# Narrowing a third of the gated layer's weights beside the attention and keeping them in DRAM

## The chip, the cores and the metric

One Trainium2 chip, one of its cores. The metric is device time in microseconds of one execution; below it stands as the median of three runs, beside one execution that was profiled. The engines are called TensorE (PE in the profile, its weight loads PEld), VectorE (DVE), ScalarE (ACT), GpSimd (POOL) and SyncE (SP, which here only issues DMAs).

## What is computed

Attention in both directions between 512 rows and 32 states for 8 x 8 heads of 64, then a mixture of eight experts with one expert per row, then a gated layer (`moe2`):

```python
attn_out = _attn_ref(**attn_kwargs)                  # (8, 8, 544, 64)
x = attn_out.transpose(0, 2, 1, 3).reshape(4608, 512)
# experts: argmax of normalised logits, out[mask] = gate * relu(x[mask] @ w1[e]) @ w2[e]
x = _moe_ref(x=x, **moe_kwargs)
# gated layer, d_ff = 1536
g = x @ w_gate
silu = g * (1.0 / (1.0 + np.exp(-g)))
val = x @ w_val
out = (silu * val @ w_out).astype(np.float32)
```

The three weights of the gated layer arrive as float64 (`wide` in the code), as pairs of 32-bit words. The kernel has no float64 arithmetic: it narrows a tile to float32 by integer operations on the two words.

## The kernel before

Each product is made of three float32r matmuls (`mm3`, lines 138 to 140), for which every operand is split into a high and a low part (`split`: ScalarE copies the high part, line 127; VectorE or GpSimd subtracts for the low one, line 131).

**Order.** The order of all instructions is made by hand. `Streams` runs a main stream and several side streams: each `yield` of the main stream is one round, in which every side stream takes one step; a side stream that yields a number k sits out k rounds, and one that yields a function stands until it is true. `groups` is the first main stream: 64 expert rounds n (8 for each of 8 batches b), each with the products `ph` (then `hH` on ScalarE, `hL` on VectorE, lines 616 and 617) and, for the round before, `acc`; the weights of experts are fetched on SP and split in between, and every other round has `states_w1`. An expert round has about 7 yields; n = 0 has four fewer than the others of its kind. Beside it run `attn_a` for two halves q (lines 244 to 319; the last is started once batch 5 has begun, sits out `a_off` rounds, and adds one to `done_a` at its end), `attn_b`, `route`, and `later`.

**later** (line 1054) waits until all 16 parts of `attn_a` are done, closes their pool `ap`, routes the state rows (`slots_route`), then runs `weights2` and after it the experts of the state rows (`slots`), which run beside the rest of the gated layer.

**weights2** (line 878) prepares 36 tiles: for each f of 12 the tiles g, v and o (128 x 512). A tile is loaded on SP (line 895, 512 KB, three raw buffers), squared on ScalarE (line 918), narrowed by four VectorE instructions (`narrow`, lines 871, 873, 875, 876), and split one iteration later, the low part on GpSimd. `c_gap` sets the rounds between: 4 while experts run, 2 once `w2b` is open. From f = 2 on a tile also waits for a function, which costs a round.

**moe2** (line 956) is the second main stream: 8 units of 512 rows and one of 256, each with 12 steps f of pg, pv and, for the step before, o: 36 matmuls of 512 columns and 12 yields. A step can be placed only when its three tiles have been split. During the first unit the tiles of f = 4 to 11 are still being made; as long as they are, the low part `yL` of the product is made on GpSimd, else on VectorE. The buffer `sg` is single.

Of the kernel before, what the change touches and what calls it, by code (L numbers as in the profile page):

```python
# [9 lines left out]
F32 = mybir.dt.float32  # L10
F32R = mybir.dt.float32r
BF16 = mybir.dt.bfloat16
I32 = mybir.dt.int32
AF = mybir.ActivationFunctionType
# [12 lines left out]
NCA = 2  # L27
# [53 lines left out]
class W:  # L81
# [25 lines left out]
    c_mask = "vector"  # L107
    c_gap = (0, 4, 2)
    c_lo = ("pool",)


class Kernel:
# [30 lines left out]
    def setup(self, cp, kp, dp):  # L143
        nc = self.nc
        for i in range(2):
            self.zp.tile([128, 512], F32, tag="sst", name=f"sst{i}", bufs=2)
        self.bds = [[cp.tile([128, 2, 128], F32, name=f"bd{q}_{i}") for i in range(NBD)] for q in range(2)]
        for i in range(NBD):
            for q in range(2):
                nc.vector.memset(self.bds[q][i], 0.0)  # L150
        for q in range(2):
            self.load_bd(0, q)
            self.load_x(0, q)
        for q in range(2):
            self.load_bd(1, q)
        self.tauv = cp.tile([128, 32], F32, name="tauv")[:, 0:1]
        nc.sync.dma_start(self.tauv, self.tau.to_broadcast([128, 1]))
        self.em = self.zp.tile([8, DM], F32, tag="sq", name="em", bufs=2)
        nc.sync.dma_start(self.em, self.emb)
        self.ident = kp.tile([128, 128], F32, name="ident")  # L160
        make_identity(nc, self.ident)
        self.bs = [[cp.tile([128, 2, 128], F32R, name=f"bs{k}{q}") for k in "HL"] for q in range(2)]
        one = self.zp.tile([128, 512], F32, tag="sq", name="one", bufs=2)[:, :128]
        nc.gpsimd.memset(one, 1.0)
        self.ones = kp.tile([128, 128], F32R, name="ones")
        nc.vector.tensor_copy(self.ones, one)
        self.rev = cp.tile([128, 4, 8], F32, name="rev")
        for e in range(E):
            nc.gpsimd.memset(self.rev[:, :, e:e + 1], float(E - e))
        kc = cp.tile([128, 2], F32, name="kc")  # L170
        nc.gpsimd.memset(kc[:, 0:1], 0.5)
        nc.gpsimd.memset(kc[:, 1:2], math.e)
        self.half = kc[:, 0:1]
        self.euler = kc[:, 1:2].unsqueeze(2)
        self.enT = cp.tile([128, 4, 16], F32R, name="enT")
        self.tri_b = cp.tile([128, 128], BF16, name="tri_b")
        self.ones_b = cp.tile([128, 128], BF16, name="ones_b")
        self.iota = self.zp.tile([128, 512], F32, tag="iota", name="iota", bufs=1)
        self.rtau = cp.tile([128, 1], F32, name="rtau")
        self.ess = cp.tile([8, 1], F32, name="ess")  # L180
        self.en = cp.tile([8, 1], F32, name="en")

        cp.tile([128, 32], F32, name="fill_c")
        self.xs = [self.zp.tile([128, DM], F32, tag="xs", name=f"xs{t}", bufs=2) for t in range(2)]
        self.goh = kp.tile([128, 36, 8], F32, name="goh")
        self.ov = kp.tile([128, 9], F32, name="ov")
        self.ovi = kp.tile([128, 10], I32, name="ovi")
        kp.tile([128, 24], F32, name="fill_k")
        self.x2d = dp.tile([9, 128, 4, 512], F32, name="x2d")
        self.x1d = dp.tile([9, 2, 128, 4, 512], F32R, name="x1d")  # L190
        self.ec = kp.tile([128, NCHK], I32, name="ec")
        self.gm8 = kp.tile([128, 256], F32, name="gm8")
        self.xsld = dp.tile([NCHK, 128, 512], F32R, name="xsld")
        self.seltd = dp.tile([128, 1024], F32R, name="seltd")
        self.x2sd = dp.tile([2, 128, 4, 512], F32R, name="x2sd")
        self.gohd = dp.tile([9, 128, 4, 8], F32, name="gohd")
        self.gm, self.eb, self.scS, self.bdT, self.at, self.PT, self.ss = {}, {}, {}, {}, {}, {}, {}
# [664 lines left out]
            yield W.s_gap[2]  # L862


    def narrow(self, raw, t, q):

        nc = self.nc
        lo, hi = raw[:, :, 0], raw[:, :, 1]  # L870
        getattr(nc, W.c_mask).scalar_tensor_tensor(t.bitcast(F32), t.bitcast(F32), LEAST_SQ, hi.bitcast(F32),  # L871
                                       op0=ALU.is_ge, op1=ALU.mult)
        nc.vector.tensor_scalar(q, t, 3, 0x3FFFFFFF, op0=ALU.logical_shift_left, op1=ALU.bitwise_and)  # L873
        yield W.c_gap[0]
        nc.vector.scalar_tensor_tensor(t, t, -0x40000000, q, op0=ALU.bitwise_and, op1=ALU.bitwise_or)  # L875
        nc.vector.scalar_tensor_tensor(q, lo, 29, t, op0=ALU.logical_shift_right, op1=ALU.bitwise_or)  # L876

    def weights2(self):

        nc, cv = self.nc, self.cv  # L880
        todo = [(f, nm) for f in range(NC2) for nm in "gvo"]
        N = len(todo)
        raw, sq, val = {}, {}, {}

        def load(i):
            if i >= N:
                return
            f, nm = todo[i]
            fs = slice(f * 128, f * 128 + 128)
            k = " k" if self.wide else ""  # L890
            src = {"g": self.wg, "v": self.wv, "o": self.wo}[nm]
            src = src[fs] if nm == "o" else src[:, fs].rearrange(f"(c p) f{k} -> p c f{k}", p=128)
            shape = [128, 512, 2] if self.wide else [128, 512]
            raw[i] = cv.tile(shape, I32 if self.wide else F32, tag="raw", name=f"raw{nm}{f}", bufs=3)
            nc.sync.dma_start(raw[i] if nm == "o" else raw[i].rearrange(f"p (c f){k} -> p c f{k}", c=4), src)

        load(0)
        load(1)
        yield 4
        for i in range(N + 2):  # L900
            m = i - 2
            if m >= 0:
                f, nm = todo[m]
                if f < NCA:
                    h, l = [self.w2a.tile([128, 512], F32R, tag=f"{nm}{k}{f}", name=f"{nm}{k}{f}") for k in "HL"]
                elif f < NCA + NCT:
                    yield lambda: not self.routing
                    tags = TAKEN[2 * (m - 3 * NCA):][:2]
                    h, l = [self.zp.tile([128, 512], F32R, tag=t, name=f"{nm}{k}{f}", bufs=BUFS[t])
                            for k, t in zip("HL", tags)]  # L910
                else:
                    yield lambda: self.w2b is not None
                    h, l = [self.w2b.tile([128, 512], F32R, tag=f"{nm}{k}{f}", name=f"{nm}{k}{f}") for k in "HL"]
                self.split(h, l, val.pop(m), lo_eng=W.c_lo[m % len(W.c_lo)])
                self.W2.setdefault(f, []).extend((h, l))
            if i < N and self.wide:
                sq[i] = cv.tile([128, 512], I32, tag="t64", name=f"t{i}", bufs=2)
                nc.scalar.activation(sq[i].bitcast(F32), raw[i][:, :, 1].bitcast(F32), AF.Square)
            m = i - 1
            if 0 <= m < N:  # L920
                if self.wide:
                    q = cv.tile([128, 512], I32, tag="q64", name=f"q{m}", bufs=2)
                    yield from self.narrow(raw.pop(m), sq.pop(m), q)
                    val[m] = q.bitcast(F32)
                else:
                    val[m] = raw.pop(m)
            load(i + 2)
            yield W.c_gap[1 if self.w2b is None else 2]
# [81 lines left out]
    def run(self):  # L1010
# [9 lines left out]
        def close(*keys):  # L1020
            for k in keys:
                open_.pop(k).close()
# [11 lines left out]
        cp = pool("cp", 1, "right")  # L1034
        self.wp = pool("wp", 2, "right")
        self.hp = pool("hp", 2, "right")
        self.raw, self.regs, self.fetched, self.cuts, self.done_a, self.xr = {}, {}, [0, 0], [0, 0], 0, {}
        self.en_done = self.scored = False
        st = Streams()
        self.spreading, self.slots_done, self.begun = False, False, set()  # L1040
        self.W2, self.x2, self.x2r, self.w2b, self.routing = {}, [], {}, None, True
# [6 lines left out]
        def routes():  # L1048
# [2 lines left out]
                yield from self.route(b)  # L1051
            self.routing = False

        def later():

            yield lambda: self.done_a == 16
            close("ap")
            self.lp = pool("lp", reuse_waits="tile")
            yield from self.slots_route()
            close("lp")  # L1060
# [33 lines left out]
        with tc.manual_schedule():  # L1094
            self.setup(cp, kp, dp)
            for q in range(2):
                st.add(self.start_pace(self.attn_a(q), W.p_a))
            st.add(self.start_pace(attn_b(), W.p_b))
            st.add(self.setup_route())
            st.add(self.start_pace(routes(), W.p_r))  # L1100
            st.add(later())
            st.run(main())
        close("lp", "x2p", "gp", "ps")
        self.general(pool, close)
# [119 lines left out]
```

## Time and profile before

| | us |
|---|---|
| median of 3 runs | 1520.24 (1518.88 to 1521.37) |
| the profiled execution | 1522.9 |
| its span, first to last instruction | 1521.4 |
| PE busy | 1423.9 (94%) |
| DVE busy | 853.0 (56%) |
| ACT busy | 572.9 (38%) |
| POOL busy | 284.3 (19%) |

The shares are means over stages that differ. In the page's 40 slices of 38 us each TensorE's digit is 9 nearly throughout; it is 7 or 8 only in slices 12 to 18, and 4 and 6 in the first two. VectorE's digit is 5 to 8 up to slice 13, 9 in the next four, 8 in slice 18, and 2 to 4 after it, mostly. Of the DMA traffic, 120.91 of 132.53 MB goes through the queue of SP.

### The profile page before, as it was taken

What the parts mean: (1) busy time and instruction counts of PE and PEld (TensorE: products, weight loads), DVE (VectorE), ACT (ScalarE), POOL (GpSimd) and SP (SyncE); (2) the same over time, 40 slices, a digit from 0 to 9 for tenths busy, and PEclk for the clock granted to TensorE, in tenths of its full rate; (3) what the DMA queues carried; (4) which work ended last, traced back from release to release, by engine and by line L of the source; (5) the groups of instructions that cost most, each with busy time, mean ns of one, the idle gap of its engine ahead of it and who ended that gap; (6) DMA issues with size and microseconds to landing.
All of it is one profiled execution on the core that took longest, in us unless ns stands there. A gap on an engine that the chain in (4) does not pass through costs nothing.

```text
span 1521.4 us, 20615 instructions
## 1 busy us (share of the span) xinstructions
PE 1423.9 (94%) x6997; PEld 1167.1 (77%) x6998; DVE 853.0 (56%) x1725; ACT 572.9 (38%) x1195; POOL 284.3 (19%) x254
## 2 busy tenths in 40 slices
PE   4699999999988788889999999999999999999997
PEld 4577877878877576668888888888888888888887
DVE  5568687677785999984443444344344443443232
ACT  3455554544644433333332333233242332332121
POOL 2224334343343335430000000000000000000100
PEclk8799999999999999999999999999999999999999
DMA  3333233333244543332222132132131231231210
GB/s 75 100 83 107 90 113 121 103 106 104 71 145 144 173 134 111 125 112 72 60 70 76 60 90 77 42 101 65 36 111 49 62 105 41 74 94 35 90 40 16
DMA packets 134818, 132.53 MB, mean 87 GB/s; under 512 B 45736, under 2 KB 109736, under 8 KB 134448
## 3 DMA queue, kind: packets, MB, share of 16 engines
q1 hardware_dynamic: 128992, 120.91, 26.2%
q0 software_dynamic: 5520, 9.96, 2.4%
q8 instruction: 57, 0.93, 0.3%
q14 instruction: 57, 0.47, 0.1%
q10 hardware_dynamic: 192, 0.26, 0.1%
HBM read 108.54 MB, written 31.98 MB: 92 GB/s over the span
## 4 chain that ended last, share of the span: by engine, by line
PE 53%; DVE 10%; issue 2%; DMA 2%; ACT 1%; POOL 1%; SPq 0%; DVEq 0%; ACTq 0%; POOLq 0%
PE pg L138 5%; PE pv L138 5%; PE pg L139 5%; PE pg L140 5%; PE o L140 5%; PE o L139 5%; PE pv L139 5%; PE pv L140 5%; PE o L138 5%; DVE t L875 2%; DVE t L871 2%; DVE q L873 2%; PE psl L803 1%; DVE q L876 1%; PE psl L804 1%
## 5 line engine op out<-in xcount | busy, mean ns | idle before, releaser
L138 PE MATMUL pg<-x2H,gH 128*128 128x512 f32 (+1 forms) x432 | 167.6, 388 | 12.6 <-DVE sg L985 12.4
L985 DVE TENSOR_TENSOR sg<-pg,sg 128x512 f32<-128x512 f32 (+1 forms) x108 | 71.4, 661 | 182.1 <-ACT sg L984 181.8
L138 PE MATMUL pv<-x2H,vH 128*128 128x512 f32 (+1 forms) x432 | 166.0, 384 | 3.1 <-DVE sg L987 3.1
L139 PE MATMUL pg<-x2L,gH 128*128 128x512 f32 (+1 forms) x432 | 166.0, 384 | 0.2 <-DVE x2L L131 0.2
L140 PE MATMUL pg<-x2H,gL 128*128 128x512 f32 (+1 forms) x432 | 165.9, 384 | 0.0
L140 PE MATMUL pv<-x2H,vL 128*128 128x512 f32 (+1 forms) x432 | 164.8, 381 | 0.0
L139 PE MATMUL pv<-x2L,vH 128*128 128x512 f32 (+1 forms) x432 | 164.7, 381 | 0.0
L140 PE MATMUL o<-oH,yL 128*128 128x512 f32 x408 | 160.5, 393 | 0.0
L139 PE MATMUL o<-oL,yH 128*128 128x512 f32 x408 | 160.3, 393 | 0.0
L138 PE MATMUL o<-oH,yH 128*128 128x512 f32 x408 | 160.3, 393 | 0.0
L127 ACT ACTIVATE yH<-sg 128x512 fp32r<-128x512 f32 (+1 forms) x108 | 65.7, 609 | 237.1 <-DVE sg L987 237.1
L131 DVE TENSOR_TENSOR swL<-sraw,swH 128x256 fp32r<-128x256 f32 x256 | 102.7, 424 | 52.8 <-ACT swH L127 51.1
L984 ACT ACTIVATE sg<-pg 128x512 f32<-128x512 f32 (+1 forms) x108 | 61.9, 573 | 184.8 <-PE pg L140 181.1
L127 ACT ACTIVATE swH<-sraw 128x256 fp32r<-128x256 f32 x256 | 99.3, 410 | 63.5 <-PE sacc L830 38.2
L139 PE MATMUL acc<-hL,w1H 128*128 128x512 f32 x256 | 103.4, 404 | 15.1 <-DVE hL L617 15.1
L138 PE MATMUL acc<-hH,w1H 128*128 128x512 f32 x256 | 107.1, 418 | 9.5 <-ACT w1H L127 9.1
L987 DVE TENSOR_TENSOR sg<-pv,sg 128x512 f32<-128x512 f32 (+1 forms) x108 | 71.3, 660 | 76.6 <-PE pv L140 76.1
L140 PE MATMUL acc<-hH,w1L 128*128 128x512 f32 x256 | 103.4, 404 | 1.5 <-DVE w1L L131 0.9
L138 PEld LDWEIGHTS pg<-x2H,gH 128*128 128x128 f32 x432 | 81.8, 189 | 29.6 <-DVE sg L985 15.8
L131 DVE TENSOR_TENSOR yL<-sg,yH 128x512 fp32r<-128x512 f32 (+1 forms) x98 | 64.7, 660 | 65.9 <-ACT yH L127 65.9
L138 PEld LDWEIGHTS pv<-x2H,vH 128*128 128x128 f32 x432 | 81.3, 188 | 18.4 <-DVE sg L987 4.5
L140 PEld LDWEIGHTS pg<-x2H,gL 128*128 128x128 f32 x432 | 82.0, 190 | 17.1
(290 smaller groups left out, 3014.3 us busy)
## 6 DMA issues: line engine op xcount, KB each, us to landing
sraw<-in_moe_w SPq DMA_DIRECT2D x256, 128.0 KB
raw<-in_moe_w SPq DMA_DIRECT2D x32, 512.0 KB
raw<-in_moe_w SPq DMA_DIRECT2D x64, 256.0 KB
xr<-in_x SPq DMA_DIRECT2D x64, 128.0 KB
x2d<-xo SPq DMA_DIRECT2D x32, 256.0 KB
x2r<-x2d SPq DMA_DIRECT2D x32, 256.0 KB
out<-ob SPq DMA_DIRECT2D x32, 256.0 KB
rawg<-in_moe_w_gate SPq DMA_DIRECT2D x12, 512.0 KB
```

The costliest lines, as they stand in the source:

```text
L127: nc.scalar.activation(hi, src, AF.Copy)
L131: eng.tensor_sub(lo, src, hi.bitcast(F32))
L138: nc.tensor.matmul(ps, ah, bh, start=first and i == 0, stop=False)
L139: nc.tensor.matmul(ps, ah, bl, start=False, stop=False)
L140: nc.tensor.matmul(ps, al, bh, start=False, stop=last and i == n - 1)
L803: nc.tensor.matmul(ps[:, :256], x[:, c, :], wH, start=c == 0, stop=False)
L871: getattr(nc, W.c_mask).scalar_tensor_tensor(t.bitcast(F32), t.bitcast(F32), LEAST_SQ, hi.bitcast(F32), op0=ALU.is_ge, op1=ALU.mult)
L873: nc.vector.tensor_scalar(q, t, 3, 0x3FFFFFFF, op0=ALU.logical_shift_left, op1=ALU.bitwise_and)
L875: nc.vector.scalar_tensor_tensor(t, t, -0x40000000, q, op0=ALU.bitwise_and, op1=ALU.bitwise_or)
L984: nc.scalar.activation(sg, pg, AF.Sigmoid)
L985: nc.vector.tensor_mul(sg, pg, sg)
L987: nc.vector.tensor_mul(sg, pv, sg)
```

## The change

The o tiles of all 12 f are narrowed by a side stream of their own, `narrow_early`, which starts with the first expert round. It has a pool `ep` (one raw buffer, two results), loads a raw tile on SP, squares it on ScalarE 13 rounds later, narrows it with the same four VectorE instructions in two pairs (the intermediate now goes into every other word of the raw tile), and 7 rounds after the last of them stores the result on SP into a DRAM array `w32`. `later` also waits for its end before it closes the pools. In `weights2` an o tile is now loaded from `w32` on GpSimd's queue (256 KB) into a raw buffer, isn't squared or narrowed, and is split one iteration earlier than before. `cut` and `load_w` hold code that stood in `weights2`.

```diff
+    n_begin, n_gap, n_step = 0, 12, (2, 2, 6)
...
+        self.w32 = dp.tile([NC2, 128, 512], F32, name="w32")
...
-    def narrow(self, raw, t, q):
+    def narrow(self, raw, t, q, gap=None, out=None):
...
-        yield W.c_gap[0]
+        yield W.c_gap[0] if gap is None else gap
         nc.vector.scalar_tensor_tensor(t, t, -0x40000000, q, op0=ALU.bitwise_and, op1=ALU.bitwise_or)
-        nc.vector.scalar_tensor_tensor(q, lo, 29, t, op0=ALU.logical_shift_right, op1=ALU.bitwise_or)
+        nc.vector.scalar_tensor_tensor(q if out is None else out, lo, 29, t, op0=ALU.logical_shift_right, op1=ALU.bitwise_or)
...
+    def narrow_early(self):
+
+        nc, ep = self.nc, self.ep
+        yield lambda: len(self.begun) > W.n_begin
+        for i in range(NC2):
+            raw = self.load_w(ep, i, "o", 1)
+            yield W.n_gap
+            sq = ep.tile([128, 512], I32, tag="t64", name=f"te{i}", bufs=2)
+            nc.scalar.activation(sq.bitcast(F32), raw[:, :, 1].bitcast(F32), AF.Square)
+            yield W.n_step[0]
+            yield from self.narrow(raw, sq, raw[:, :, 1], W.n_step[1], sq)
+            yield W.n_step[2]
+            nc.sync.dma_start(self.w32[i], sq.bitcast(F32))
...
+        early = {i for i, (f, nm) in enumerate(todo) if self.wide and nm == "o"}
...
+            if i in early:
+                t = cv.tile([128, 512, 2], I32, tag="raw", name=f"raw{nm}{f}", bufs=3)
+                raw[i] = t.rearrange("p f k -> p (f k)")[:, :512].bitcast(F32)
+                nc.gpsimd.dma_start(raw[i], self.w32[f])
+            else:
+                raw[i] = self.load_w(cv, f, nm, 3)
...
             m = i - 2
-            if m >= 0:
...
+            if m >= 0 and m not in early:
+                yield from cut(m)
+            if i < N and self.wide and i not in early:
                 sq[i] = cv.tile([128, 512], I32, tag="t64", name=f"t{i}", bufs=2)
...
             m = i - 1
             if 0 <= m < N:
-                if self.wide:
+                if m in early:
+                    val[m] = raw.pop(m)
+                    yield from cut(m)
+                elif self.wide:
...
-            yield lambda: self.done_a == 16
-            close("ap")
+            yield lambda: self.done_a == 16 and self.narrowed
+            close("ap", "ep")
```

## Rows read from the trace of the kernel before

**Rows 1.** Busy time (operations) by engine in stretches; clock, DMA share, GB/s.
```profile
core 0: us, PE busy (x) PEld busy (x) DVE busy (x) ACT busy (x) POOL busy (x), PEclk, DMA share, GB/s
72.00:404.00 332.00, 314.61 (x1751) 263.98 (x1751) 240.98 (x550) 171.33 (x339) 128.04 (x91) 0.98 0.34 100
...
500.00:557.90 57.90, 47.24 (x194) 35.63 (x195) 54.24 (x77) 26.87 (x49) 20.10 (x14) 0.94 0.53 160
557.90:664.40 106.50, 91.67 (x379) 71.24 (x377) 99.54 (x119) 40.12 (x69) 52.84 (x34) 0.98 0.41 131
```
**Rows 2.** Chain that ended last, from 557 to 600 us, shares by line.
```profile
by line: DVE t L875 19.7%; DVE t L871 18.8%; DVE q L873 17.6%; issue 12.7%; DVE q L876 9.1%; DVE sg L987 6.0%; DVE sg L985 5.8%; POOL yL L131 4.0%; ACT sg L984 2.5%; DVE xo L637 1.6%; ACT t L918 1.5%; ACT yH L127 1.5%; DVEq L873 0.4%; ACT v
```
**Rows 3.** VectorE in order of time, a g tile: start, duration, line, operation.
```profile
489.07 0.69 DVE L871 SCALAR_TENSOR_TENSOR t<-t,rawg 128x512 f32<-128x512 f32 x1
489.80 0.43 DVE L873 TENSOR_SCALAR q<-t 128x512 int32<-128x512 int32 x1
490.25 0.69 DVE L875 SCALAR_TENSOR_TENSOR t<-t,q 128x512 int32<-128x512 int32 x1
490.98 0.69 DVE L876 SCALAR_TENSOR_TENSOR q<-rawg,t 128x512 int32<-128x512 int32 x1
```
**Rows 4.** The same view, a product and an o tile in the first unit.
```profile
624.25 0.68 DVE L987 TENSOR_TENSOR sg<-pv,sg 128x512 f32<-128x512 f32 x1
624.85 0.68 DVE L871 SCALAR_TENSOR_TENSOR t<-t,rawo 128x512 f32<-128x512 f32 x1
625.63 0.43 DVE L873 TENSOR_SCALAR q<-t 128x512 int32<-128x512 int32 x1
626.09 1.67 DVE L875 SCALAR_TENSOR_TENSOR t<-t,q 128x512 int32<-128x512 int32 x1
627.79 1.67 DVE L876 SCALAR_TENSOR_TENSOR q<-rawo,t 128x512 int32<-128x512 int32 x1
```
**Rows 5.** The fourth o tile in time, and tile rawo (ns min/median/max, starts).
```profile
557.89 0.88 DVE L871 SCALAR_TENSOR_TENSOR t<-t,rawo 128x512 f32<-128x512 f32 x1
...
L918 ACT ACTIVATE t<-rawo x12: 644/658/672, 493.2 to 660.8; 128x512 f32<-128x512 f32 x12
L871 DVE SCALAR_TENSOR_TENSOR t<-t,rawo x12: 678/684/1791, 503.9 to 664.3; 128x512 f32<-128x512 f32 x12
```
**Rows 6.** TensorE's waits, 557.9 to 664.4 us: total us, times, longest.
```profile
PE pg L138 <- DVE sg L985: 9.8, 6, 2.9
PE pv L138 <- DVE sg L987: 3.1, 4, 1.0
```
**Rows 7.** TensorE in order of time, first and last of 24 matmuls.
```profile
656.75 0.39 PE L138 MATMUL pv<-x2H,vH 128*128 128x512 f32 x1
...
662.08 0.39 PE L140 MATMUL o<-oH,yL 128*128 128x512 f32 x1
```
**Rows 8.** Tile hL, first and last start; VectorE in order of time.
```profile
L617 DVE SCALAR_TENSOR_TENSOR hL<-ph,hH x64: 627/683/692, 71.3 to 551.5; 128x512 fp32r<-128x512 f32 x64
...
500.73 0.68 DVE L617 SCALAR_TENSOR_TENSOR hL<-ph,hH 128x512 fp32r<-128x512 f32 x1
```
**Rows 9.** TensorE's longest group of waits on VectorE, 72 to 404 us.
```profile
PE acc L139 <- DVE hL L617: 8.2, 4, 2.4
```
**Rows 10.** Busy time as in rows 1, three stretches beside the attention.
```profile
120.00:160.00 40.00, 38.32 (x223) 32.15 (x222) 33.29 (x65) 21.60 (x42) 17.91 (x14) 1.00 0.34 100
160.00:200.00 40.00, 39.02 (x222) 33.40 (x221) 27.31 (x71) 17.02 (x36) 14.34 (x12) 1.00 0.30 90
...
360.00:400.00 40.00, 36.68 (x202) 30.57 (x201) 31.17 (x58) 20.11 (x37) 21.36 (x16) 1.00 0.30 93
```
**Rows 11.** ScalarE in order of time: the 46th hH, and the slots' routing.
```profile
414.81 0.59 ACT L616 ACTIVATE hH<-ph 128x512 fp32r<-128x512 f32 x1
...
418.23 0.63 ACT L127 ACTIVATE xsHL<-xs 128x512 fp32r<-128x512 f32 x1
```
**Rows 12.** Tile sx: loads issued on GpSimd, ns min/median/max; time to landing.
```profile
L791 POOL DMA_DIRECT2D sx<-xsld x8: 535/562/622, 671.0 to 1275.9; - x8
...
DMA to landing us min/median/max: 3.0/3.2/3.6
```

More of the change, by code (lines that the diff above doesn't have):

```diff
@@ L873, in narrow, with load_w @@
         nc.vector.tensor_scalar(q, t, 3, 0x3FFFFFFF, op0=ALU.logical_shift_left, op1=ALU.bitwise_and)
-        yield W.c_gap[0]
+        yield W.c_gap[0] if gap is None else gap
         nc.vector.scalar_tensor_tensor(t, t, -0x40000000, q, op0=ALU.bitwise_and, op1=ALU.bitwise_or)
-        nc.vector.scalar_tensor_tensor(q, lo, 29, t, op0=ALU.logical_shift_right, op1=ALU.bitwise_or)
+        nc.vector.scalar_tensor_tensor(q if out is None else out, lo, 29, t, op0=ALU.logical_shift_right, op1=ALU.bitwise_or)
+    def load_w(self, pool, f, nm, bufs):
+        fs = slice(f * 128, f * 128 + 128)
+        k = " k" if self.wide else ""
+        src = {"g": self.wg, "v": self.wv, "o": self.wo}[nm]
+        src = src[fs] if nm == "o" else src[:, fs].rearrange(f"(c p) f{k} -> p c f{k}", p=128)
+        shape = [128, 512, 2] if self.wide else [128, 512]
+        raw = pool.tile(shape, I32 if self.wide else F32, tag="raw", name=f"raw{nm}{f}", bufs=bufs)
+        self.nc.sync.dma_start(raw if nm == "o" else raw.rearrange(f"p (c f){k} -> p c f{k}", c=4), src)
+        return raw
+    def narrow_early(self):
[10 more added lines that the diff above has]
+            nc.sync.dma_start(self.w32[i], sq.bitcast(F32))
     def weights2(self):
@@ L888, in load, with cut @@
             f, nm = todo[i]
[L889 to L895, printed above, removed]
+            if i in early:
[4 more added lines that the diff above has]
+                raw[i] = self.load_w(cv, f, nm, 3)
+        def cut(m):
+            f, nm = todo[m]
+            if f < NCA:
+                h, l = [self.w2a.tile([128, 512], F32R, tag=f"{nm}{k}{f}", name=f"{nm}{k}{f}") for k in "HL"]
+            elif f < NCA + NCT:
+                yield lambda: not self.routing
+                tags = TAKEN[2 * (m - 3 * NCA):][:2]
+                h, l = [self.zp.tile([128, 512], F32R, tag=t, name=f"{nm}{k}{f}", bufs=BUFS[t])
+                        for k, t in zip("HL", tags)]
+            else:
+                yield lambda: self.w2b is not None
+                h, l = [self.w2b.tile([128, 512], F32R, tag=f"{nm}{k}{f}", name=f"{nm}{k}{f}") for k in "HL"]
+            self.split(h, l, val.pop(m), lo_eng=W.c_lo[m % len(W.c_lo)])
+            self.W2.setdefault(f, []).extend((h, l))
         load(0)
@@ L901, in weights2 @@
             m = i - 2
-            if m >= 0:
[L903 to L916, printed above, removed]
+            if m >= 0 and m not in early:
+                yield from cut(m)
+            if i < N and self.wide and i not in early:
                 sq[i] = cv.tile([128, 512], I32, tag="t64", name=f"t{i}", bufs=2)
@@ L1036, in run @@
         self.hp = pool("hp", 2, "right")
+        self.ep = pool("ep", 1, "right")
         self.raw, self.regs, self.fetched, self.cuts, self.done_a, self.xr = {}, {}, [0, 0], [0, 0], 0, {}
-        self.en_done = self.scored = False
+        self.en_done = self.scored = self.narrowed = False
         st = Streams()
@@ L1052, in routes, with narrow_early @@
             self.routing = False
+        def narrow_early():
+            if self.wide:
+                yield from self.narrow_early()
+            self.narrowed = True
         def later():
-            yield lambda: self.done_a == 16
-            close("ap")
+            yield lambda: self.done_a == 16 and self.narrowed
+            close("ap", "ep")
             self.lp = pool("lp", reuse_waits="tile")
@@ L1101, in run @@
             st.add(later())
+            st.add(narrow_early())
             st.run(main())
```

## The prediction

> **What bounds the kernel now.** I read three views in order: the stretches by engine, the chain of waits inside the stretch that looked worst, and the instructions of the engine it named. [Rows 1] split the part that the change touches into three. Beside the attention (72 to 404 us) TensorE is busy 314.61 of 332 us and VectorE 240.98, 73%: TensorE leads, with room on VectorE. In the last expert rounds (500 to 557.9) VectorE is busy 54.24 of 57.9 us, 94%, and TensorE falls to 82%. In the first unit of the gated layer (557.9 to 664.4) VectorE is busy 99.54 of 106.5, 93%, and TensorE 86%. The chain of that stretch confirms it [rows 2]: four lines of `narrow`, all VectorE, hold most of it. So narrowing is paid there nearly one for one, and most of it is free, or nearly so, earlier. The change moves a third of it.
>
> The unit of the sum is one narrowed tile. Undisturbed it takes from 489.07 to 491.67, 2.60 us [rows 3]. Disturbed, the same four instructions take 4.6 us [rows 4]: two of them run 1.67 us instead of 0.69, 0.98 more each. The last stretch has the GpSimd's 34 operations beside it, 52.84 us [rows 1], 1.55 us each. Eight f are 24 tiles at 2.60 us and 20 products at 0.60 (from 624.25 to 624.85 [rows 4]), 74.4 of 106.4 us; the other 32, spread over 34 GpSimd operations, are 0.94 us each, about what one long instruction adds. I count that much of VectorE per GpSimd operation.
>
> TensorE's own floor comes from [rows 7]: the first and the last of 24 back-to-back matmuls, 23 intervals in 5.33 us, 0.232 us each. One step of the gated layer is 36 of them, 8.34 us.
>
> **Part 1: twelve narrowings leave the late stage.** Eight of them lie between the o tile at 557.9 and the one at 664.3 [rows 5]: 106.4 us, 13.3 us for one f (three tiles). By the code these took 15 rounds of the schedule per f: each tile has one round for the wait on `w2b`, one inside `narrow`, three for the gap. A step of the gated layer is 12 rounds, so 120 rounds are 10 steps, whose floor is 83.4 us; 23 us are lost. With the change an f takes 14 rounds (the o tile has no narrow round, and the splitting of o moves one iteration ahead). VectorE then has per f: 13.3, less 2.6 for the o tile, less a twelfth of a step's own two products and one GpSimd `yL` (about 0.2), so 10.5 us. The GpSimd's share stays, because the o tile is still split there. Eight f come to 84 us, still above the floor of 112 rounds (77.8): VectorE remains the limit, less tightly. Of the 22.2 us saved, 5.6 go back, since 8 rounds of TensorE work (0.67 step) are still to be done afterwards. Net 16.6 us. Ends: 8 us, if the 23 us of loss shrink only in proportion to the narrowing (one in three), and 23 us, if TensorE reaches its floor. I take 16.6, since the busy share and the chain both say that VectorE sets the pace.
>
> Three more o tiles lie in the last expert rounds. From 500.7 to 551.5 [rows 8] there are 8 rounds of 18 matmuls and three sets of 12 half-size ones, 162 in full ones, 37.5 us at the floor: 13.3 us are lost in 50.8. Three tiles are 7.8 us of a VectorE that is 94% busy. Some of the loss is weights that land late, which this doesn't mend. I take 6, ends 0 and 7.8. The twelfth (664.3) ends the stretch; I count it at nothing, ends 0 and 2.6.
>
> **Part 2: the same twelve beside the attention.** Each is the same four VectorE instructions. The intermediate is now written with a stride, so its 0.43 us instruction may become one of 0.69 us like its neighbours [rows 3]: 2.60 to 2.86 us, 31 to 34 us in all, and more where a GpSimd operation meets them (the GpSimd is busy 128 of 332 us [rows 1]), up to some 46. I take 34. They come every 26 rounds (13 after the load, 3, 3, 7). The first hL is at 71.3 us [rows 8], and the 46th hH at 414.8 [rows 11], so an expert round of 7 is 7.6 us and a round 1.09 us: twelve tiles spread from 72 to about 412 us, one in 28 us. VectorE rises from 73% to 83%.
>
> What a microsecond of VectorE costs there: on average little, TensorE's longest group of waits on it is 8.2 us [rows 9] against 241 us of VectorE, 0.03 per us, 1 us in all. At the margin more: [rows 10] show VectorE at 27.31 with TensorE at 39.02 (160 to 200), 33.29 with 38.32 (120 to 160), 31.17 with 36.68 (360 to 400): slopes 0.12 and 0.61, mean 0.36, 12 us in all. These stretches differ in more than VectorE's load, so I take a price between, 0.24: 8 us. The cover is that hL of one round is needed only a round later; if that is used up, the price goes to 1 (first rival).
>
> ScalarE's twelve squares (0.66 us each [rows 5], 8 us) go into an engine busy 171 of 332 us: nothing. They can only hold ScalarE if the raw tile is late, and it has 13 rounds, 14 us, to land.
>
> **Part 3: queues and waits.** SP gets twelve 512 KB loads earlier and twelve 256 KB stores more. Each store waits for the last narrowing instruction, and behind it on SP are the next raw load and the expert weights of the following rounds; it is issued 7 rounds (7.6 us) after that instruction was put into VectorE's queue, so it should find it done. Traffic rises by 9.4 MB over 340 us, 28 GB/s on 100, share 0.34 to about 0.44: nothing, ends 0 and 3 us (the weights' landing is on the path at times). In the late stage SP loses a third of its raw loads, each of which stands there until a raw buffer has been narrowed; the x2r fetches behind them can only gain.
>
> GpSimd gets twelve loads of 256 KB. The nearest row: it issues its loads of that size in 0.56 us, and they land in 3.0 to 3.6 us [rows 12]. Eight in the stretch are 4.5 us on top of 52.84, of about 84: 68%. Each goes out two tiles (about 10 rounds) ahead of its use. I take nothing, ends 0 and 5 us.
> A rule speaks against this. The Trainium skill, "SBUF — State Buffer" (the box on the trap "DVE blocks DMA"), says that descriptors of a load issued on GpSimd can't be written while VectorE runs in a two-port mode, and gives 620 ns alone and 3100 ns overlapped; an estimate by it would be 2.5 us more for each of eight loads, 20 us of GpSimd time. No run here shows such a load beside a saturated VectorE; the third rival below is that mechanism.
>
> The new condition for closing the attention's pool: the last store is emitted in round 313 after the first expert round begins. The last attention stage ends, by the code, in round 276 + 40 = 316 plus whatever rounds the main stream spends waiting, which count for both. So the gate is open three rounds before; the slots' routing, now at 418.2 [rows 11], doesn't move. If it were late, it would cost about 1 us a round.
>
> **The sum.** -16.6 - 6 + 8 = -14.6 us. The profiled execution took 1522.9 us (span 1521.4, 1.5 around it), so 1508.3 for it; the median of the runs is 1520.24, 2.7 below, and I state the forecast against the median: 1505.6, rounded to 1506. With every unknown at one end the sum reaches from -32 to +12; they won't all fall one way.
>
> **The rivals.**
> First, slower: VectorE saturates beside the attention. For it: 120 to 160 us is at 33.29 of 40, and a tile and a half (4.3 us) brings it to 37.6, 94%, the level at which the late stretches lose time one for one. Against it: other stretches stay near 32. If all 34 us count at 1, the sum is +34 - 22.6, 1532; it is slower by over 3 us from a price of 0.75 on. Chance 0.12.
> Second, TensorE reaches its floor in the late stage, and the price beside the attention is a tenth: -23 - 7.8 + 3, 1492. For it: with gaps between narrowings, GpSimd operations meet fewer VectorE ones. Against: the GpSimd has as many operations as before, in less time. Chance 0.18.
> Third, the loads on GpSimd hold it. Each longer issue stands ahead of a `yL`, on which the next sigmoid waits (one buffer). If each of eight is held for one long VectorE instruction, 1.67 us [rows 4], of which half is slack, that is 6.7 us; the sum becomes -7.9, 1512. Chance 0.08.
> Fourth, nothing comes of it: the loss in the late stage moves to the next thing (TensorE's waits there on VectorE's products are only 9.8 + 3.1 us [rows 6], and ScalarE, GpSimd and VectorE hand each tile on in turn); the gain is the low end, 8, and the attention takes it back: 1520. Chance 0.08.
>
> **How the numbers follow.** The forecast has 0.54. Its own bounds, with the second and third rival, reach from 1491 to 1522, which leaves out most of the first rival and the tail of the second. A difference under 0.2% (3 us) can't be told from none here. Faster by more: the forecast, the second and the third, 0.80. Within: the fourth, 0.08. Slower: the first, 0.12.
>
> **What would show it.** In the trace after: between the o tiles' splits in the first unit about 10.5 us instead of 13.3, and its end some 20 us earlier relative to the end of the experts; VectorE in the late stage still above 90%; beside the attention VectorE at 83% and TensorE's waits on hL, bdL grown by a few us; the experts' last hL about 2 us later or earlier than 551.5; GpSimd's loads near 0.56 us; the slots' routing at about 418 plus what the attention lost. Wrong would be: 72 to 404 us of work stretched by over 15 us, GpSimd loads of 2 us or more, or a first unit as long as before.

## The result, and the profile after

| | before | after |
|---|---|---|
| median, us | 1520.03 (4 runs) | 1539.84 (1538.18 to 1541.15, 4 runs) |
| span of the profiled execution, us | 1521.4 | 1538.9 |
| VectorE busy over the span, us | 853.0 | 853.2 |

The changed kernel is slower: ratio 1.0122, 95% interval 1.0104 to 1.014, some 20 us. VectorE does the same work in total, as it should when work is only moved. Two places in the trace make most of it: 30.7 us lost beside the attention less 14.7 gained in the first unit are 16.0, of the 17.5 by which the span grew.

The bill came beside the attention. The slots' routing, at 418.23 before [rows 11], starts at 448.8: 31 us later. Busy time by engine, with the columns of [rows 1] and in stretches that answer to its three, each some 31 us later (the attention, the last expert rounds, the first unit while its weights are made):

```profile
core 0: us, PE busy (x) PEld busy (x) DVE busy (x) ACT busy (x) POOL busy (x), PEclk, DMA share, GB/s
72.00:435.00 363.00, 324.86 (x1751) 271.43 (x1750) 276.16 (x596) 178.02 (x351) 128.07 (x91) 0.95 0.38 117
...
530.80:588.20 57.40, 49.65 (x206) 38.11 (x207) 47.09 (x66) 25.09 (x46) 22.14 (x18) 0.94 0.49 155
...
588.20:677.30 89.10, 81.45 (x339) 63.91 (x338) 75.10 (x85) 35.82 (x60) 52.11 (x40) 0.98 0.41 128
```

The same 1751 matmuls that took 332 us take 363. VectorE has 35.2 us more, as forecast (34). TensorE's idle time grew from 17.4 to 38.1 us, 20.7 more, and its busy time from 314.61 to 324.86, 10.3 more for the same matmuls: 31 us together. The second part goes with the clock, granted at 0.95 in the mean instead of 0.98.

The gain came in the first unit. The first sigmoid product of that unit and the first of the next, in order of time on VectorE, in the kernel before:

```profile
560.68 0.68 DVE L985 TENSOR_TENSOR sg<-pg,sg 128x512 f32<-128x512 f32 x1
...
681.94 0.68 DVE L985 TENSOR_TENSOR sg<-pg,sg 128x512 f32<-128x512 f32 x1
```

and after:

```profile
591.42 0.69 DVE L1017 TENSOR_TENSOR sg<-pg,sg 128x512 f32<-128x512 f32 x1 [2.40 <-ACT sg L1016]
...
697.95 0.69 DVE L1017 TENSOR_TENSOR sg<-pg,sg 128x512 f32<-128x512 f32 x1
```

121.3 us became 106.5: 14.7 us gained. Between the routing and the first product nothing was gained: the one is 30.6 us late, the other 30.7.

What TensorE waited for, 72 to 435 us (waited on, us in total, times, longest); [rows 9] had 8.2 us as the longest group:

```profile
PE acc L140 <- DVE hL L619: 12.3, 4, 4.7
PE pt L274 <- DVE bdL L132: 5.4, 5, 1.4
PE pb L267 <- DVE hL L619: 5.4, 2, 2.9
PE px L141 <- DVE atL L132: 5.3, 1, 5.3
PE pat L368 <- DVE xT L132: 3.6, 1, 3.6
```

All are low parts that VectorE makes: the waits are on VectorE's queue. Of these five groups, 32.0 us, the kernel before had 14.8: besides the 8.2 on hL these (it had none on xT):

```profile
PE pt L272 <- DVE bdL L131: 4.1, 5, 1.2
PE pb L265 <- DVE hL L617: 1.4, 3, 0.5
PE px L140 <- DVE atL L131: 1.1, 1, 1.1
```

So 17.2 us came on top, 8.1 of them on hL and 9.1 on the attention's own low parts. One wait read through, that of px on atL. VectorE in order of time:

```profile
91.53 1.61 DVE L877 SCALAR_TENSOR_TENSOR te<-te,rawo 128x512 int32<-128x512 int32 x1
93.17 2.71 DVE L878 SCALAR_TENSOR_TENSOR te<-rawo,te 128x512 int32<-128x512 int32 x1
95.81 0.68 DVE L619 SCALAR_TENSOR_TENSOR hL<-ph,hH 128x512 fp32r<-128x512 f32 x1
96.41 1.28 DVE L132 TENSOR_TENSOR w0L<-raw,w0H 128x512 fp32r<-128x512 f32 x2
97.61 0.68 DVE L132 TENSOR_TENSOR atL<-pat,atH 128x512 fp32r<-128x512 f32 x1
```

GpSimd at that time:

```profile
91.29 1.30 POOL L132 TENSOR_TENSOR w1L<-raw,w1H 128x512 fp32r<-128x512 f32 x1 [2.49 <-ACT w1H L128]
92.72 2.61 POOL L132 TENSOR_TENSOR xrL<-xr,xrH 128x1024 fp32r<-128x1024 f32 x1
```

and TensorE (in square brackets the idle time before, and what ended it):

```profile
98.34 0.58 PE L141 MATMUL px<-bsH,atL 128*128 128x256 f32 x1 [5.34 <-DVE atL L132]
98.72 0.63 PE L472 MATMUL pg<-dgH,ones 128*128 128x512 f32 x1
99.15 0.63 PE L472 MATMUL pg<-dgL,ones 128*128 128x512 f32 x1
...
102.29 0.40 PE L139 MATMUL ph<-atH,swH 128*128 128x512 f32 x1
```

A tile's second pair, 1.4 us undisturbed [rows 3], meets two GpSimd operations and takes 4.3. `atL`, behind it in the queue with three instructions between, is late by as much, and TensorE stands 5.34 us where it stood 1.10 before. After the gap the matmuls of 512 columns follow each other at 0.43 us, at a granted clock of 0.53 of full speed from 98.3 to 102.2, the lower of the clock's two levels (1.2 GHz), before they return to the 0.23 of the upper one (2.4 GHz) at 102.29. The Trainium skill, "SBUF — State Buffer", section "Who interferes with whom", says that a VectorE instruction with two SBUF inputs and a GpSimd instruction that reads SBUF exclude each other for the whole instruction; these rows agree, 2.71 us instead of 0.69 beside a GpSimd operation of 2.61.

### The profile page after: what moved, and what is told of

The parts are those of the page before. It is cut to its first block, busy times and chain, and to the rows that moved or that the text cites. A ratio compares the mean times of both kernels' runs of the same rounds, so it can differ in the third digit from the quotient of the medians.

```text
span 1538.9 us, 20605 instructions
## 1 busy us (share of the span) xinstructions
PE 1432.0 (93%) x6997; PEld 1173.8 (76%) x6998; DVE 853.2 (55%) x1726; ACT 572.9 (37%) x1195; POOL 284.9 (19%) x265
## 4 chain that ended last, share of the span: by engine, by line
PE 54%; DVE 7%; DMA 2%; issue 2%; ACT 1%; POOL 1%; SPq 0%; DVEq 0%; ACTq 0%; POOLq 0%
PE pg L139 6%; PE pv L139 6%; PE pg L141 5%; PE pg L140 5%; PE pv L141 5%; PE pv L140 5%; PE o L141 5%; PE o L140 5%; PE o L139 5%; DVE t L877 1%; PE psl L805 1%; DMA x2r<-x2d 1%; PE psl L806 1%; DVE t L873 1%; PE sacc L833 1%
## 5 line engine op out<-in xcount | busy, mean ns | idle before, releaser
L140 PE MATMUL acc<-hL,w1H 128*128 128x512 f32 x256 | 104.8, 409 | 16.0 <-DVE hL L619 15.9
L141 PEld LDWEIGHTS pv<-x2H,vL 128*128 128x128 f32 x432 | 81.3, 188 | 17.1
```

The source lines that it names most:

```text
L140: nc.tensor.matmul(ps, ah, bl, start=False, stop=False)
L141: nc.tensor.matmul(ps, al, bh, start=False, stop=last and i == n - 1)
```

## The experiments

Each kernel ran against the kernel before on the same chip; "above" and "below" are differences of those medians, in us. The first four rested on one theory and two rivals. Theory: VectorE's narrowing, standing in its queue ahead of low parts that TensorE needs at once, costs the 31 us; where in the batch it stands sets the price. First rival: SP's queue, the transfers or ScalarE's squares cost it. Second rival: each microsecond of VectorE costs the same there.

**The early part alone.**

```diff
-        early = {i for i, (f, nm) in enumerate(todo) if self.wide and nm == "o"}
+        early = set()
```

> The early narrowing runs as in the changed kernel, but its result isn't used: the late stage loads and narrows all 36 tiles as before. This is the attention's part of the bill alone. By the traces of before and after, the 46th hH comes 31 us later and nothing else of the early part should cost: 1551 us (1546 to 1556). If part of the 31 us came from the other change (the gate, the pools), it is below 1540.

Measured 1555.02 us against 1523.52, 31.5 above, ratio 1.0207 (1.0184 to 1.0229). The early part's bill stands by itself.

**The late part alone.**

```diff
-            if self.wide:
-                yield from self.narrow_early()
             self.narrowed = True
...
-                nc.gpsimd.dma_start(raw[i], self.w32[f])
+                nc.gpsimd.dma_start(raw[i], self.w2[f // 8, f % 8 * 128:f % 8 * 128 + 128, :])
```

> No early narrowing at all; the late stage loads float32 tiles of 256 KB on GpSimd from another weight array (so the out-projection is computed with wrong weights) and splits them one iteration earlier, as in the changed kernel. This is the gain alone. By the traces the first unit is 14.5 us shorter and the last expert rounds 1 us: 1505 us (1502 to 1509). If the late gain were hidden behind the late start, as a buffer effect, it would be different by over 5 us.

Measured 1512.37 us against 1523.52, 11.2 below, 0.9924 (0.9897 to 0.9952). Expected were 1502 to 1509 us: as a time a miss; as a difference from the 1520 of the kernel before, 11 to 18 below, just inside. 31.5 less 11.2 is 20.3, and the whole change cost 19.8: the two halves add up. The gain lies in the first unit, as in the changed kernel: its first product comes at 561.0 us, where it was before, the second unit's at 667.9 instead of 681.94.

**The early part without VectorE.**

```diff
-            yield from self.narrow(raw, sq, raw[:, :, 1], W.n_step[1], sq)
+            yield W.n_step[1]
```

> The changed kernel without the four VectorE instructions of each early tile (so the out-projection's weights are wrong): raw loads, ScalarE's squares, stores, gate and the late part all stay. If VectorE's narrowing costs the 31 us, only the late gain is left: 1505 to 1509 us. If SP's queue, the DMA traffic or ScalarE's squares cost it, about 1535 to 1540.

Measured 1512.24 us, 11.3 below, 0.9924 (0.9896 to 0.9953): the median of the late part alone. Twelve loads and stores on SP, 9.4 MB of traffic, twelve squares and the gate cost no more than the uncertainty of these runs, some 5 us (the time itself is above the expected 1505 to 1509, as the late part's was above its own; in its profiled execution the routing starts at 423.2, 4.8 us later than in the late part alone). The first rival can't carry the 31 us; they come only with VectorE's four instructions.

**The same at fixed places.** Each batch has 56 rounds. With a period of 26 the tiles wander through it; by the starts of the 64 hH in both traces, the delay of the changed kernel grew by 2 to 7 us from each of the first seven tiles to the next, to 27.9 us, and by some 2 us in all with the next four, which stood near rounds 27 to 31 and 53 to 57 of a batch.

```diff
+        yield 9
-        for i in range(NC2):
+        for i in range(NC2 - 1):
...
-            yield W.n_step[2]
+            yield 8 if i < NC2 - 2 else 3
...
-        early = {i for i, (f, nm) in enumerate(todo) if self.wide and nm == "o"}
+        early = {i for i, (f, nm) in enumerate(todo) if self.wide and nm == "o" and f < NC2 - 1}
```

> The early narrowing at fixed places: period 28 rounds instead of 26, so that each batch of 56 rounds has its two tiles at the same two places, rounds 27 and 55 of it, where in the changed kernel's trace four tiles cost 2 us together; eleven tiles early, the twelfth late as before. If the place within the batch sets the price: 8 to 12 us paid for 13 us gained, 1515 us (1509 to 1521). If each microsecond of VectorE costs the same anywhere beside the attention (31 us for 35): 27 us paid, 1534 us.

Measured 1517.70 us, 5.8 below, 0.9966 (0.995 to 0.9982), and in the last run below once more, 2.5 below, 0.9979 (0.9966 to 0.9991): faster than both kernels. With eleven twelfths of the late gain (10.3), eleven tiles cost 4.5 us in the first pair of medians and 7.8 in the second; in the trace the routing starts at 422.2, 3.9 us later than in the kernel before. The second rival is out. In this kernel no narrowing instruction was lengthened; tile rawo (ns minimum, median, maximum, of one instruction; starts):

```profile
L873 DVE SCALAR_TENSOR_TENSOR te<-te,rawo x11: 679/683/691, 103.0 to 407.4; 128x512 f32<-128x512 f32 x11
L875 DVE TENSOR_SCALAR rawo<-te x11: 427/428/430, 103.7 to 408.1; 128x512 int32<-128x512 int32 x11
L877 DVE SCALAR_TENSOR_TENSOR te<-te,rawo x11: 680/681/684, 107.3 to 411.4; 128x512 int32<-128x512 int32 x11
L878 DVE SCALAR_TENSOR_TENSOR te<-rawo,te x11: 691/692/694, 108.0 to 412.1; 128x512 int32<-128x512 int32 x11
```

The same tile in the changed kernel, with maxima up to 2711 ns (and GpSimd's twelve loads):

```profile
L873 DVE SCALAR_TENSOR_TENSOR te<-te,rawo x12: 628/688/1784, 89.9 to 429.5; 128x512 f32<-128x512 f32 x12
L875 DVE TENSOR_SCALAR rawo<-te x12: 427/429/2448, 90.6 to 431.3; 128x512 int32<-128x512 int32 x12
L877 DVE SCALAR_TENSOR_TENSOR te<-te,rawo x12: 628/682/1611, 91.5 to 435.5; 128x512 int32<-128x512 int32 x12
L878 DVE SCALAR_TENSOR_TENSOR te<-rawo,te x12: 691/693/2711, 93.2 to 436.2; 128x512 int32<-128x512 int32 x12
L919 POOL DMA_DIRECT2D rawo<-w x12: 559/559/707, 520.2 to 668.7; - x12
```

**The same period, 14 rounds earlier.** This asks whether it was the place or the regular period.

```diff
-            yield W.n_gap
+            yield W.n_gap if i else 8
```

(this beside the edits of the run before, but without its first `yield 9`)

> As the run at fixed places (period 28, eleven tiles early), but 14 rounds earlier, so that the tiles fall on rounds 13 and 41 of each batch, near places where the changed kernel lost 2 to 4 us a tile. If the place sets the price: 25 to 45 us early and about 10 gained late, 15 to 35 us above the kernel before. If the regular period is what helped: as the run at fixed places, 6 us below it.

Measured 1546.71 us against 1523.63, 23.1 above, 1.0144 (1.0108 to 1.018). Eleven tiles at these places cost 33.4 us, at the other two places 4.5 to 7.8. TensorE's waits, 72 to 438 us:

```profile
PE pat L368 <- DVE xT L132: 18.2, 5, 3.6
PE acc L140 <- DVE hL L619: 6.4, 4, 2.4
```

The first line is the same wait of 3.64 us, five times, once in each of five batches. One of them, on VectorE:

```profile
159.62 2.45 DVE L875 TENSOR_SCALAR rawo<-te 128x512 int32<-128x512 int32 x1
162.00 0.68 DVE L132 TENSOR_TENSOR xT<-pt,xT 128x512 fp32r<-128x512 f32 x1
```

GpSimd and TensorE at that time:

```profile
157.54 1.50 POOL L359 TENSOR_TENSOR ex<-ex,s 128x512 f32<-128x512 f32 x1
159.01 2.78 POOL L132 TENSOR_TENSOR xrL<-xr,xrH 128x1024 fp32r<-128x1024 f32 x1
...
162.82 1.09 PE L368 MATMUL pat<-ident,ex 128*128 128x128 f32 x4 [3.64 <-DVE xT L132]
```

The 0.43 us instruction takes 2.45 beside a GpSimd operation of 2.78, directly ahead of the low part of the transposed x. The matmul that stands doesn't read xT: its operand `ex` was ready at 159.04. By the code, pat and the pt from which xT is made take their buffers from one pool of four in PSUM (`pa`; pb, px, ph and psw are from it too), and such a buffer comes free when the low part has been made from it. So a low part can hold TensorE in two ways, as an operand (atL for px) and as the last reader of a buffer; that pat waited for just this buffer is read from code and times, and no run tested it.

The two runs at fixed places differ in both things at once. The eleven tiles' instructions took 40.0 us here and 27.3 there, so the places of this run also met GpSimd; per microsecond that VectorE was busy with them, the price is 0.83 here and 0.16 to 0.29 there.

**What part is the lengthening?** Four maxima instead of the four narrowing instructions: about as long, one SBUF input each.

```diff
-            yield from self.narrow(raw, sq, raw[:, :, 1], W.n_step[1], sq)
+            for j in range(4):
+                if j == 2:
+                    yield W.n_step[1]
+                nc.vector.reduce_max(ep.tile([128, 1], F32, tag="dum", name=f"dum{i}_{j}", bufs=1), sq.bitcast(F32), axis=AX.X)
```

> The changed kernel, with the four VectorE instructions of each early tile replaced by four maxima over the squares (0.69 us each by rows of the trace, one SBUF input; so nothing is narrowed and the out-projection's weights are wrong), in the same rounds. VectorE's plain time stays (2.7 us a tile), but these have one input, and GpSimd's operations should not lengthen them; in the changed kernel the four took 40.1 us instead of the 27.3 that undisturbed ones take. If VectorE's queue alone is the price: the same 31 us early, so 20 us above the kernel before. If the lengthening beside GpSimd's operations is what hurts: the early part falls to 10 to 20 us, so 1 below to 9 above it.

Measured 1533.05 us, 9.4 above, 1.0053 (1.0026 to 1.008), at the upper edge of the second expected range. Tile te shows that none was lengthened:

```profile
L903 DVE TENSOR_REDUCE dum<-te x48: 628/686/689, 88.4 to 426.9; 128x1 f32<-128x512 f32 x48
```

The early bill falls from 31 to 20.6 us for about 33 us of VectorE (48 of 0.69). So the lengthening beside GpSimd is worth some 10 us of it, within the few us of uncertainty of both runs, and VectorE time at these places, without it, some 20. The number of inputs alone doesn't explain which instructions are lengthened: L875 has one input too, and grew from 0.43 to 2.45 us.

**Single instructions, three rounds apart.**

```diff
-    n_begin, n_gap, n_step = 0, 12, (2, 2, 6)
+    n_begin, n_gap, n_step = 0, 9, (1, 2, 4)
...
+        if out is not None:
+            yield 2
         nc.vector.tensor_scalar(q, t, 3, 0x3FFFFFFF, op0=ALU.logical_shift_left, op1=ALU.bitwise_and)
...
+        if out is not None:
+            yield 2
         nc.vector.scalar_tensor_tensor(q if out is None else out, lo, 29, t, op0=ALU.logical_shift_right, op1=ALU.bitwise_or)
```

> The changed kernel with the four narrowing instructions of a tile issued singly, three rounds apart, instead of in two pairs (period still 26 rounds). If a pair ahead of a late low part makes the gap, single ones do half of it: the early part falls from 31 to 15 to 20 us, 5 to 9 us above the kernel before. If VectorE's total time sets the price: no difference from the changed kernel, 18 to 20 us above.

Measured 1534.39 us, 10.8 above, 1.0069 (1.0043 to 1.0094): the early bill is 22 us instead of 31, a little more than expected. This run also moves the instructions by up to four rounds, so smaller pieces and other places aren't told apart in it. Less lengthening is not the reason: the twelve tiles' instructions took 39.9 us, against 40.1 in the changed kernel.

**Why the last expert rounds gained nothing.** In the late part alone ScalarE's waits from 500 to 562 us have these two lines:

```profile
ACT t L947 <- DMA rawv<-in_moe_w_val: 5.0, 2, 2.5
ACT oH L128 <- PE ph L141: 4.7, 1, 4.7
```

I suspected the second: the o split, one iteration earlier than before, writes into a buffer that the last products `ph` still read. The edit, beside those of the late part alone:

```diff
-                t = cv.tile([128, 512, 2], I32, tag="raw", name=f"raw{nm}{f}", bufs=3)
-                raw[i] = t.rearrange("p f k -> p (f k)")[:, :512].bitcast(F32)
+                t = cv.tile([128, 512], I32, tag="rawo", name=f"raw{nm}{f}", bufs=2)
+                raw[i] = t.bitcast(F32)
...
-                raw[i] = self.load_w(cv, f, nm, 3)
+                raw[i] = self.load_w(cv, f, nm, 2)
...
-            if m >= 0 and m not in early:
+            if m >= 0:
                 yield from cut(m)
...
                     val[m] = raw.pop(m)
-                    yield from cut(m)
```

> The late part alone as in the run without early narrowing (weights of another array, so the out-projection is wrong), but with the o tile split two iterations after its load's turn, as g and v are, not one, out of a buffer of its own. In that run ScalarE stood 4.7 us at an o split whose target TensorE still read, late in the expert rounds, and these gained nothing up to the first unit. If that wait ate the gain: 14 to 17 us below the kernel before. If something else did (weights that land late, the last batch's routing): as that run, 11 us below.

Measured 1505.48 us, 18.1 below, 0.9874 (0.9851 to 0.9898). It looks like a hit, but the wait that I blamed is still there, and longer:

```profile
ACT oH L128 <- PE ph L141: 5.8, 1, 5.8
```

So that reason falls, whatever the gain is. The two kernels had been on different chips; both again on one:

> The late part alone, once more, on the same chip as the run below it (the two were on different chips): 11 us below the kernel before (8 to 14).

Measured 1510.94 against 1523.37, 12.4 below, 0.9902 (0.9871 to 0.9932).

> The late part alone with the later o split, beside the run above on one chip. If the later split is worth what the two chips showed: 7 us less than the run above, 18 below the kernel before. If it is worth what it was worth beside early narrowing: 3 to 4 us less. If it was the chip: no difference.

Measured 1507.44, 15.9 below, 0.9905 (0.9873 to 0.9937). The medians differ by 3.5 us, the ratios not at all: on one chip the later split is worth between nothing and some 3.5 us, and at least half of the 7 us between the first two runs was not the split.

**Both together.** The fixed places and the later split in one kernel (its one late o tile is loaded an iteration later), and beside it the fixed places alone again.

> The run at fixed places and the later o split together: eleven tiles early at rounds 27 and 55 of each batch, o split two iterations after its load's turn out of a buffer of its own, the twelfth tile narrowed late as before (its load one iteration later). If the two effects add: 4.5 us paid early, 11/12 of 18.1 gained late, 11 to 13 us below the kernel before (ratio 0.992). If the later split only helped because no early tiles were there: as the run at fixed places, 6 below.

Measured 1514.37 against 1520.26, 5.9 below, 0.9951 (0.9932 to 0.997); expected were 11 to 13, a miss. It is the fastest of the kernels that compute everything; by the ratios to the kernel before, 26 us below the changed one.

> The run at fixed places once more, beside the one above on the same chip: 6 us below the kernel before (3 to 8).

Measured 1517.79 on the same chip, 2.5 below, 0.9979 (0.9966 to 0.9991); expected were 3 to 8. The later split adds some 3 us here, at the edge of what the intervals can tell. The expected 11 to 13 took 18.1 for the late gain, from the other chip, and 4.5 for the bill. With the 15.9 of the repeat, eleven twelfths of it 14.6, and the bill of 7.8, the sum is 6.8, and 5.9 was measured: no more is needed to explain the miss.

## Why the prediction was wrong

**Where VectorE is the limit: right in the mechanism, short in size.** The first unit is VectorE's, and taking a third of the narrowing out gains there: 14.7 us between the two products; at the end of the span 11 to 15 of it are left in the runs of the late part alone. The forecast was 16.6 net (106.4 less 84 is 22.4, not 22.2; nothing hangs on it). The fourth and the twelfth split of an o tile on GpSimd, before:

```profile
561.50 1.61 POOL L131 TENSOR_TENSOR oL<-q,oH 128x512 fp32r<-128x512 f32 x1 [3.28 <-ACT oH L127]
...
669.77 1.29 POOL L131 TENSOR_TENSOR oL<-q,oH 128x512 fp32r<-128x512 f32 x1 [3.60 <-ACT oH L127]
```

and after:

```profile
586.64 1.30 POOL L132 TENSOR_TENSOR oL<-rawo,oH 128x512 fp32r<-128x512 f32 x1
...
677.34 1.30 POOL L132 TENSOR_TENSOR oL<-rawo,oH 128x512 fp32r<-128x512 f32 x1 [0.62 <-ACT oH L128]
```

Eight steps of three tiles took 108.3 us, 13.5 each, and take 90.7, 11.3 each; the forecast was 10.5. So 17.6 us were saved here instead of 22.4, and VectorE was busy 84% of the stretch, not above 90% as forecast.

**The last expert rounds: wrong.** I took 6 us, from VectorE's 94%. VectorE fell to 47.09 of 57.4 us, 82%, and TensorE, by the first product, gained nothing: its waits of acc on hL fell from 6.8 us (500 to 558) to 3.6 (530 to 590), those on ScalarE's `w1H` rose from 1.9 to 3.5, and ScalarE now stood 3.9 us for the raw tile of v, a wait that the trace before doesn't have there. That these took the gain is argued, not shown. The relief went into the tiles: their fourth o split came 25.1 us later, the routing 30.6, so they were 5.4 us further on when the first unit began. There the lead was paid out: 5.4 and 17.6 are 23.0 us, of which 8.4 went back, since TensorE had 20.6 us from the last o split to the second unit's product instead of 12.2. The late part as a whole had 22.6 forecast and gave 14.7. The busy share of a stretch named the engine, but not what ends the waits of TensorE when it is relieved. I had put 0 as the low end for these rounds, and it was 0.

**VectorE's added work: right in size.** 35.2 us more, forecast 34. The strided intermediate costs nothing (0.43 us as before). The twelve tiles' instructions took 40.1 us in the changed kernel; the eleven at fixed places took 27.3, or 29.8 for twelve, so some 10 us are lengthening.

**Its price: the step that failed.** "I take a price between, 0.24: 8 us" was a mean over a whole stretch. Measured: 31 us for 35, 0.88. The step before it is what misled: "that hL of one round is needed only a round later". That cover failed for hL itself, on which TensorE's waits grew by 8.1 us (12.3 and 5.4 after, 8.2 and 1.4 before), and it never held for the attention's `atL`, `xT` and `bdL`, whose waits grew by 9.1 us: TensorE needs those, or the buffer they are made from, within the same few instructions. The average price, 0.03, counted the longest group alone; with the other three that the trace before already had, 14.8 us, it was 0.06, and the names of the low parts that matter stood there. The slopes of [rows 10] compared stretches, in which the attention's phases are mixed; they can't show that two places of a batch differ by a factor of four to seven. The runs at fixed places did: 4.5 to 7.8 us and 33.4 us for the same eleven tiles. The prediction's own sign of being wrong, the attention's work stretched by over 15 us, came true at twice that.

**The clock was missing.** A third of the bill, 10.3 of 31 us, is longer matmuls, at the lower clock level after gaps. The trace before had this after its own gaps, and the sum had no term for it.

**The rivals.** "VectorE saturates beside the attention" gave 1532 and a chance of 0.12. The result, 1540, lies on its side, and its mechanism isn't what happened: VectorE was busy 276 of 363 us, 76%, and the bill came without saturation. A price near 1 doesn't need a full engine, only an instruction in the wrong place of the queue. The third rival, loads on GpSimd held by VectorE, is out: the loads took 0.56 us to issue (0.707 at most) and 3.0 in the median to land, as in [rows 12], beside a VectorE at 82 to 84%. The trap that the Trainium skill names on its page "SBUF — State Buffer" didn't show here. The gate, SP's queue, the traffic and ScalarE's squares were costed at nothing, and without VectorE's part they cost nothing that the runs can tell from it.

**What stays open.** What, after the change, holds the stretch from the last expert rounds to the first product; why one tile's place costs more than another's beyond what it meets on GpSimd, as the waits are read through for two places only; and what it is in an instruction, beside the number of its inputs, that lets GpSimd lengthen it.

## What to carry to other kernels

Work moved under a stage that another engine leads isn't priced by the free share of the engine that takes it, but by what stands behind it in that engine's queue, and by what it meets on a third engine: follow one period of the stage, mark the instructions whose result, or whose buffer, the leading engine takes at once, and put the moved work elsewhere. Work with another period than the stage's (26 rounds against 56 here) wanders through good and bad places; lock it to the stage, and at a good place, for a locked bad one costs more than wandering (33.4 us for eleven tiles against 31 for twelve). And the price of a gap is not the gap alone: in this kernel's stage half as much again was lost on longer matmuls.

## What was not expected of the hardware

What a gap of TensorE costs after it has ended: behind the 5.34 us that ended at 98.34 seven intervals of 512 columns were 0.43 us instead of 0.23 (granted clock 0.53), behind the 2.00 us that ended at 664.48 in the kernel before seven as well (0.51 from 665.3 to 668.7), some 1.7 us each time on top of the gap. A single VectorE instruction grew to 2.71 us (from 0.69) and, in another run, another to 2.45 (from 0.43) each beside one long GpSimd operation, while 48 maxima over the same tiles kept to 0.69 in the same rounds.
